# Seven of eight experts taken by rank of their token counts, each place with its own number of rows

## The chip, the cores and the metric

One core of a Trainium2 chip runs the whole program. The time is the device time of one execution in microseconds (us). The engines are PE (matrix products), ACT, DVE and POOL (element-wise work and index work) and SP, which issues most of the DMAs; the profile counts loads of PE's weights apart, as PEld. The median of three runs before the change is 919.82 us (919.14 to 919.92).

## The reference

Three layers follow each other on 3072 tokens (4 sequences of 768) of 384 values: a linear attention with a decaying state per head, a maximum of three products with an output product, and a mixture of eight experts in which every token goes to two. Cut to the last layer, on which the change works:

```python
noisy = x @ w_gate + log1p(exp(x @ w_noise)) * noise      # 3072 x 8
top2 = the two largest of each row; top2_w = softmax of the two
for e in range(8):
    rows = tokens that have e among their two
    h = maximum(x[rows] @ w1[e], 0)                        # 384 -> 1024
    out[rows] += weight of e * (h @ w2[e])                 # 1024 -> 384
```

With the inputs that setup_inputs() draws, this arithmetic gives the experts 799, 828, 716, 763, 766, 766, 772 and 734 tokens (expert 0 to 7), 6144 in all.

## The kernel before, in words

**The first half.** Attention and the three-product layer run over eight blocks of 384 tokens. After each block a short routing program on DVE finds each token's two experts and its place among their tokens, and six indirect DMAs of POOL (L632) write the token's 393 words (384 values, eight gate weights, its number) to a table in HBM, `XS`. Expert e owns rows 896 e to 896 e + 895 there (`CAP` is 896), and rows that no token takes hold zeros and a number past the end.

**The expert stage.** An expert's rows are done in two groups: g = 0 has its first 512 rows, g = 1 the next 320 (`GR` is 832, so a group of 832 - 512 columns). The list `groups` has the order (0,0), (0,1), (1,0), ... (7,1). The second group's columns are the same for all experts. If an expert has more than 832 rows, a flag is set, and `more_rows` does the rest after the stage.

A group goes through these steps:

- `g_load` (L694, L697): SP loads the rows into `raw`. The second group's load comes as two parts, 128 partitions with two rows each and 64 partitions with one.
- `g_tr` (L709 to L713): PE turns a tile of rows (three 128 x 128 transposes into a `b_sc` bank, of which there are two), ACT copies it rounded as `gxH`, DVE makes the rest `gxL`. Each product is done in three terms (high x high, low x high, high x low), which keeps full precision.
- `g_gate` (L722, L724): DVE copies the row numbers into `gix`, of which there are two buffers, one for each of the last two groups. The weight of the token is read where it lies, in `raw`.
- `mm1` (L734 to L736): for each of eight slices f of the hidden layer nine matmuls fill a `b_u` bank, with the group's columns moving; ACT makes `ghH` (L745), DVE `ghL` (L746). There are two `b_u` banks.
- `mm2` for g = 0 (L762 to L764): per f twelve matmuls, the tokens as weights, 384 columns moving. `mm2T` for g = 1 (L777 to L779): per f nine matmuls with `w2` as weights and the group's columns moving; the result lies turned, and `g_cols` (L788, L790) and `g_rows` (L802) turn it back, the latter inside the next expert's first step. The very last group does its eight `mm1` first and then `mm2_tile` (L815 to L817), 24 matmuls of 384 columns for each of three tiles.
- `g_out` (L827 to L833): ACT and DVE scale by the weight into `ys`, and POOL adds the rows to `out` with an indirect DMA, which reads `gix`.

**The order** is written out by hand in a loop over the groups and f = 0 to 8: `mm1(f)`, then `mm2(f - 1)`, then, from f = 3 on, the turning of one tile of the next group (`g_tr` with j = f - 3), then the conversion `e_conv` (L667 on ACT, L668 on DVE) of a piece of the next expert's weights and the load `e_load` (L654, L657) of the piece three further on; `est` has three buffers. Only the very first group differs: there the next group's rows are loaded at f = 6, its first tile is turned at f = 7 and tiles 1 and 2 at f = 8, behind `mm2(7)`. Every engine takes its instructions in the order of the program, and SP's DMAs too wait in that order. `flags` (L1011 to L1031) is a chain of small DVE operations in the first group of expert 1.

## Time and profile before

| | |
|---|---|
| median of the runs | 919.82 us |
| profiled execution, whole | 925.38 us |
| profiled execution, span of the trace | 923.6 us |
| first half and routing, up to the first expert matmul | 445.3 us |
| expert stage, first to last matmul | 445.35 to 913.50 us |
| one first group in the middle (expert 1) | 35.77 us |
| one second group in the middle (expert 1) | 22.42 us |
| after the last matmul | 10.10 us |
| PE busy over the span | 899.3 us, 97% |
| granted clock of PE, mean | 0.995 |

The profile gives each instruction its start and its duration. For PE the duration of a matmul overlaps that of the next one, so that what a matmul costs is read as the distance from one start to the next, not as its duration. A bracket at the end of a row tells how long the engine had been idle before and what released it.

### The profile page before, as it was taken

Reading aid. Unit: us, or ns where it says so; the run is one execution under the profiler, and the core shown is the slowest. Engines: PE = TensorE matmul, PEld = TensorE weight load, DVE = VectorE, ACT = ScalarE, POOL = GpSimd, SP = SyncE. Lnnn points to the kernel's source line nnn. Section 1 sums busy time; section 2 is a strip of 40 time slices with the busy share of each in tenths; the row PEclk is TensorE's granted clock in tenths of the full one; section 3 lists DMA queues with packets and bytes.
Section 4 is the critical chain, followed back from the end, with each engine's and each line's share of the span. In section 5 each row is a group of like instructions: output and inputs, shape, how many; then the busy total and the mean of one; then the engine's idle time right before and its main releaser. Section 6 shows DMA issues by size and latency. Waiting matters only on the chain.

```text
span 923.6 us, 15940 instructions
## 1 busy us (share of the span) xinstructions
PE 899.3 (97%) x6450; PEld 830.3 (90%) x6451; DVE 500.8 (54%) x1281; ACT 271.7 (29%) x555; POOL 136.5 (15%) x116
## 2 busy tenths in 40 slices
PE   7999999999999999999999999999999999999995
PEld 6767999989999999999989899998999999989895
DVE  8896876758585776747425443343433433434230
ACT  3124422212121222224124333343333433334220
POOL 1000020100202020200131121021210212102121
PEclk9999999999999999999999999999999999999998
DMA  9880332525314141123145453234531435324121
GB/s 296 265 235 2 92 109 79 192 74 170 128 51 145 48 135 40 53 72 101 53 142 139 127 122 95 68 88 109 133 89 57 101 108 138 81 62 104 41 35 18
DMA packets 46211, 96.94 MB, mean 105 GB/s; under 512 B 5937, under 2 KB 26930, under 8 KB 46130
## 3 DMA queue, kind: packets, MB, share of 16 engines
q1 hardware_dynamic: 34962, 75.89, 26.3%
q0 software_dynamic: 10624, 19.11, 9.8%
q8 instruction: 52, 0.85, 0.4%
q10 hardware_dynamic: 544, 0.85, 0.3%
q14 instruction: 29, 0.24, 0.1%
HBM read 68.79 MB, written 27.82 MB: 105 GB/s over the span
## 4 chain that ended last, share of the span: by engine, by line
PE 91%; DVE 5%; issue 2%; ACT 1%; DMA 0%; POOL 0%; POOLq 0%; ACTq 0%; DVEq 0%
PE b_u L549 8%; PE b_u L734 8%; PE b_u L735 8%; PE b_u L736 8%; PE b_u L550 7%; PE b_u L551 7%; PE b_sc L375 2%; PE b_y L399 2%; PE b_sc L709 2%; PE b_y L394 2%; PE b_u L547 2%; PE b_y L762 1%; PE b_tx L764 1%; PE b_st L762 1%; PE b_x L764 1%
## 5 line engine op out<-in xcount | busy, mean ns | idle before, releaser
L746 DVE SCALAR_TENSOR_TENSOR ghL<-b_u,ghH 128x512 fp32r<-128x512 f32 (+1 forms) x120 | 71.6, 597 | 174.7 <-ACT ghH L745 166.3
L734 PE MATMUL b_u<-gxH,e1H 128*128 128x512 f32 (+1 forms) x384 | 140.2, 365 | 0.5 <-ACT gxH L712 0.5
L833 POOL DMA_INDIRECT out_dram<-ys,gix x56 | 86.1, 1538 | 360.6 <-ACT ys L830 334.0
L549 PE MATMUL b_u<-xHt,wH 128*128 128x384 f32 x378 | 133.9, 354 | 3.3 <-issue 3.3
L735 PE MATMUL b_u<-gxL,e1H 128*128 128x512 f32 (+1 forms) x384 | 134.9, 351 | 0.2 <-DVE gxL L713 0.2
L736 PE MATMUL b_u<-gxH,e1L 128*128 128x512 f32 (+1 forms) x384 | 135.1, 352 | 0.0
L551 PE MATMUL b_u<-xHt,wl 128*128 128x384 f32 x378 | 127.5, 337 | 0.0
L550 PE MATMUL b_u<-xLt,wH 128*128 128x384 f32 x378 | 127.4, 337 | 0.0
L745 ACT ACTIVATE ghH<-b_u 128x512 fp32r<-128x512 f32 (+1 forms) x120 | 62.8, 523 | 189.1 <-PE b_u L736 180.0
L632 POOL DMA_INDIRECT XS<-rows,ii x48 | 48.0, 1000 | 418.3 <-ACT xHt L442 299.2
L736 PEld LDWEIGHTS b_u<-gxH,e1L 128*128 128x128 f32 x384 | 72.1, 188 | 8.6
L558 DVE TENSOR_TENSOR uw<-b_u,uw 128x384 f32<-128x384 f32 x96 | 53.4, 556 | 48.7 <-PE b_u L551 37.0
L549 PEld LDWEIGHTS b_u<-xHt,wH 128*128 128x128 f32 x378 | 71.0, 188 | 8.1 <-issue 4.9
L734 PEld LDWEIGHTS b_u<-gxH,e1H 128*128 128x128 f32 x384 | 72.2, 188 | 6.7 <-ACT gxH L712 0.6
L735 PEld LDWEIGHTS b_u<-gxL,e1H 128*128 128x128 f32 x384 | 72.4, 188 | 6.2 <-DVE gxL L713 0.4
L560 ACT ACTIVATE hHt<-uw 128x384 fp32r<-128x384 f32 x48 | 25.2, 525 | 157.5 <-DVE uw L558 127.1
L550 PEld LDWEIGHTS b_u<-xLt,wH 128*128 128x128 f32 x378 | 71.4, 189 | 0.0
L551 PEld LDWEIGHTS b_u<-xHt,wl 128*128 128x128 f32 x378 | 70.9, 187 | 0.0
L713 DVE TENSOR_TENSOR gxL<-b_sc,gxH 128x384 fp32r<-128x384 f32 (+1 forms) x56 | 29.4, 527 | 55.0 <-ACT gxH L712 54.9
L712 ACT ACTIVATE gxH<-b_sc 128x384 fp32r<-128x384 f32 (+1 forms) x56 | 26.1, 468 | 81.3 <-PE b_sc L709 81.3
L554 ACT ACTIVATE uw<-b_u 128x384 f32<-128x384 f32 x48 | 23.5, 489 | 53.1 <-PE b_u L551 46.5
L668 DVE TENSOR_TENSOR e1L<-est,e1H 128x768 fp32r<-128x768 f32 x32 | 30.7, 960 | 9.2 <-ACT e1H L667 8.7
(297 smaller groups left out, 1822.3 us busy)
## 6 DMA issues: line engine op xcount, KB each, us to landing
est<-in_ew_dram SPq DMA_DIRECT2D x64, 384.0 KB
ldt<-in_tm_dram SPq DMA_DIRECT2D x18, 608.0 KB
raw<-XS SPq DMA_DIRECT2D x8, 786.0 KB
wS<-in_w_dram SPq DMA_DIRECT2D x15, 384.0 KB
ldr<-in_rT_dram SPq DMA_DIRECT2D x24, 224.0 KB
ldk<-in_kT_dram SPq DMA_DIRECT2D x22, 224.0 KB
out_dram<-zrow SPq DMA_DIRECT2D x8, 576.0 KB
XS<-zrow SPq DMA_DIRECT2D x8, 393.0 KB
```

Of the source, the lines that this page charges most:

```text
L549: nc.tensor.matmul(o, WH[j][:, f, ks], xH[b][:, k, :], start=(k == 0), stop=False)
L550: nc.tensor.matmul(o, WH[j][:, f, ks], xL[b][:, k, :], start=False, stop=False)
L551: nc.tensor.matmul(o, WL[3 * f + j][:, ks], xH[b][:, k, :], start=False, stop=(k == 2))
L558: v.tensor_tensor(w, o, w, op=OP.max)
L632: st = nc.gpsimd.indirect_dma_start(out=XS, out_offset=bass.IndirectOffsetOnAxis(ap=ii[:, 3 * k + j:3 * k + j + 1], axis=0), in_=rw[:, j, ...
L668: v.tensor_sub(l_, s_, f32(h_))
L734: nc.tensor.matmul(u, a[:, k, fs], o.xH[:, k, :n], start=(k == 0), stop=False)
L735: nc.tensor.matmul(u, a[:, k, fs], o.xL[:, k, :n], start=False, stop=False)
L736: nc.tensor.matmul(u, b[:, k, fs], o.xH[:, k, :n], start=False, stop=(k == 2))
L745: nc.scalar.activation(hH[:, :n], u, AF.Relu)
L746: v.scalar_tensor_tensor(hL[:, :n], u, 0.0, f32(hH[:, :n]), op0=OP.max, op1=OP.subtract)
L833: st = nc.gpsimd.indirect_dma_start(out=out, out_offset=bass.IndirectOffsetOnAxis(ap=o.ix[P, j, :], axis=0), in_=ys[P], in_offset=None, bo ...
```

## The change

`GR` goes. `CAPS` gives each place in the order of work its own number of rows: place 0 is always expert 0 with 816; places 1 to 7 are the other seven experts sorted by falling count, with 848, 816, 800, 784, 784, 768 and 768. The second groups so have 304, 336, 304, 288, 272, 272, 256 and 256 columns in place of 320. Eight small DVE operations (`ranks`) sort the counts at the end of the routing and leave the expert of each place as a number in `nti`; SP loads it into a register, and the DMAs of weights and rows of places 1 to 7 take their address from it. As the program no longer knows which of the eight gate weights is its own, `g_gate` picks it with a product with a one-hot row (`Hot`) and a sum, into a tile `ggt`; `raw` is then not read by `g_out` any more, save for place 0. `gix` has three buffers in place of two. A second group's rows come as two equal parts where there are at most 256, else as 128, 128 and the rest. In the first group tiles 1 and 2 of the next group are turned ahead of `mm2(7)` and not behind it. On SP the load of a place's number, which waits for DVE's `nti`, stands ahead of the place's first three weight loads, and a register instruction ahead of each load. The flag for rows left over compares each place with its own number, with six small operations where one stood.

```diff
@@
 G0 = 512
 LO = 640
-GR = 832
+
+CAPS = (816, 848, 816, 800, 784, 784, 768, 768)
...
+    eidx = consts.tile([128, E], F32, name="eidx")
+    nc.gpsimd.iota(eidx, pattern=[[1, E]], base=0, channel_multiplier=0, allow_small_or_imprecise_dtypes=True)
+    capr = consts.tile([1, E], F32, name="capr")
+    for q, n in enumerate(CAPS):
+        nc.gpsimd.memset(capr[:, q:q + 1], n - (CAP - 1.0))
...
+    def ranks():
...
+        v.tensor_sub(key, Rt[:, 1:], eb[:, 0, 1:])
+        v.scalar_tensor_tensor(key, key, float(E), eidx[:, 1:], op0=OP.mult, op1=OP.subtract)
+        v.tensor_tensor(gt, key[:, None, :].to_broadcast(sh), key[:, :, None].to_broadcast(sh), op=OP.is_gt)
+        v.tensor_reduce(rank, gt, axis=AX.X, op=OP.add)
+        v.tensor_tensor(Hot[:, 1:, 1:], rank[:, None, :].to_broadcast(sh), eidx[:, :M, None].to_broadcast(sh),
+                        op=OP.is_equal)
+        v.tensor_mul(gt, Hot[:, 1:, 1:], eidx[:, None, 1:].to_broadcast(sh))
+        v.tensor_reduce(nth, gt, axis=AX.X, op=OP.add)
+        v.tensor_copy(nti[:, 1:], nth[0:1, :])
...
+            SV[e] = nc.values_load(nti[0:1, e:e + 1], engines=[mybir.EngineType.SP], min_val=1, max_val=E - 1,
...
-            nc.sync.dma_start(t.rearrange("p a c -> p (a c)"), ew1[e, i])
+            nc.sync.dma_start(t.rearrange("p a c -> p (a c)"), of(ew1, e)[i])
...
-        return G0 if g == 0 else GR - G0
...
+        return CAPS[e] - G0 if g else G0
+
+    def gparts(e, g):
+
+        if g == 0:
+            return [128] * 4
+        n = gcols(e, g)
+        return [n // 2] * 2 if n <= 256 else [128, 128, n - 256]
...
-        o.gt = o.raw[:, :, DM + e:DM + e + 1]
-        o.ix = pools[0].tile([128, 4, 1], I32, name="gix", bufs=2)
...
+        o.ix = pools[0].tile([128, 4, 1], I32, name="gix", bufs=3)
...
+            v.tensor_scalar(o.ix[:n, js], o.raw[:n, js, ROW - 1:ROW].bitcast(I32), 0.0, None, op0=OP.max)
+            if e:
+                w = [n, js.stop - js.start, E - 1]
+                v.tensor_mul(gh[:n, js, 1:], o.raw[:n, js, DM + 1:DM + E], Hot[:n, None, e, 1:].to_broadcast(w))
+                v.tensor_reduce(o.gt[:n, js], gh[:n, js, 1:], axis=AX.X, op=OP.add)
...
                 if f == 6:
                     drain(rgen)
+                    ranks()
...
+            if i == 0 and f == 8:
+                for j in range(1, len(gparts(*nxt))):
+                    g_tr(*nxt, j)
             if f > 0 and nxt:
                 (mm2T if g else mm2)(e, g, f - 1)
...
-            if nxt and (f >= 3 if i else f >= 7):
-                js = [f - 3] if i else ([0] if f == 7 else [1, 2])
...
+            j = f - (3 if i else 7)
+            if nxt and 0 <= j < (len(gparts(*nxt)) if i else 1):
+                if j == 0:
+                    g_gate(*nxt)
+                g_tr(*nxt, j)
```

On PE, at the end of the first group, before the change: the transposes of tile 0 of the next group, then `mm2(7)`, then tiles 1 and 2, then the next group's `mm1`.

```order
L709 MATMUL b_sc<-ident,raw 128x128 x2
L762 MATMUL b_y<-e2H,ghH 128x384 [waits Activation_49]
...
L764 MATMUL b_x_5256<-e2H,ghL 128x384
L709 MATMUL b_sc<-ident,raw 128x128 [waits PE_49]
L709 MATMUL b_sc<-ident,raw 128x128 x2
L709 MATMUL b_sc<-ident,raw 128x64 [waits DMAHW7_49,DVE_49]
L709 MATMUL b_sc<-ident,raw 128x64 x2
L734 MATMUL b_u<-gxH,e1H 128x320 [waits Activation_49]
```

And the same place after it (L751 is `g_tr`, L810 to L812 `mm2`, L782 `mm1`).

```order
L751 MATMUL b_sc<-ident,raw 128x128 x2
L751 MATMUL b_sc<-ident,raw 128x128 [waits PE_49]
L751 MATMUL b_sc<-ident,raw 128x128 x2
L751 MATMUL b_sc<-ident,raw 128x48 [waits DMAHW7_49,DVE_49]
L751 MATMUL b_sc<-ident,raw 128x48 x2
L810 MATMUL b_y<-e2H,ghH 128x384 [waits Activation_49]
...
L812 MATMUL b_x_5269<-e2H,ghL 128x384
L782 MATMUL b_u<-gxH,e1H 128x304 [waits Activation_49]
```

The six transposes of tiles 1 and 2, with the wait of tile 2 for DVE, have moved from behind the twelve matmuls of `mm2(7)` to ahead of them.

On DVE, in the second group of expert 0, where the row numbers of the next group are taken, before the change:

```order
L746 SCALAR_TENSOR_TENSOR ghL<-b_u,ghH 128x320 [waits Activation_49]
L722 TENSOR_SCALAR gix<-raw 128x4 [waits DMASW3_49,DMASW2_49,DMAHW3_49,DMASW1_49,DMASW0_49]
L713 TENSOR_TENSOR gxL<-b_sc,gxH 128x3x128 [waits Activation_49]
L668 TENSOR_TENSOR e1L<-est,e1H 128x3x256 [waits DMAHW4_49,Activation_49]
L746 SCALAR_TENSOR_TENSOR ghL<-b_u,ghH 128x320 [waits Activation_49]
```

And after it (DMASW are POOL's DMAs, DMAHW those of SP; L768 to L772 is `g_gate`).

```order
L794 SCALAR_TENSOR_TENSOR ghL<-b_u,ghH 128x304 [waits Activation_49]
L768 TENSOR_SCALAR gix<-raw 128x4 [waits DMAHW3_49]
L771 TENSOR_TENSOR ggh<-raw,Hot 128x4x7
L772 TENSOR_REDUCE ggt<-ggh 128x4 [waits DVE_49]
L755 TENSOR_TENSOR gxL<-b_sc,gxH 128x3x128 [waits Activation_49]
L707 TENSOR_TENSOR e1L<-est,e1H 128x3x256 [waits DMAHW4_49,Activation_49]
L794 SCALAR_TENSOR_TENSOR ghL<-b_u,ghH 128x304 [waits Activation_49]
```

The row numbers no longer wait for four DMAs of POOL, and two small operations stand behind them.

## Rows read from the trace of the kernel before

**Rows 1.** The page: busy time by engine (us, share of the span, instructions), and the chain that ended last by engine.

```profile
PE 899.3 (97%) x6450; PEld 830.3 (90%) x6451; DVE 500.8 (54%) x1281; ACT 271.7 (29%) x555; POOL 136.5 (15%) x116
...
PE 91%; DVE 5%; issue 2%; ACT 1%; DMA 0%; POOL 0%; POOLq 0%; ACTq 0%; DVEq 0%
```

**Rows 2.** Busy time by stretch (us, then busy us and instructions of PE, PEld, DVE, ACT, POOL, granted clock, DMA share, GB/s): the second group of expert 0, both groups of expert 1, and what follows the last matmul.

```profile
480.76:505.46 24.70, 23.28 (x156) 22.58 (x157) 14.99 (x26) 12.66 (x23) 6.73 (x4) 1.00 0.55 145
505.46:541.23 35.77, 35.77 (x190) 32.12 (x188) 14.90 (x38) 11.45 (x20) 5.04 (x4) 1.00 0.35 96
541.23:563.65 22.42, 22.42 (x158) 22.40 (x157) 10.65 (x19) 9.09 (x18) 5.64 (x4) 1.00 0.44 104
...
913.50:923.60 10.10, 0.00 (x1) 0.00 (x0) 0.41 (x1) 0.42 (x1) 1.42 (x1) 0.72 0.07 13
```

**Rows 3.** Timeline of PE: the first matmul of nine with 512 columns, the first of twelve with 384 columns that follow, and (second pair) the first of eighteen with 320 columns and the matmul behind them.

```profile
472.84 0.39 PE L734 MATMUL b_u<-gxH,e1H 128*128 128x512 f32 x1
...
474.94 0.34 PE L762 MATMUL b_y<-e2H,ghH 128*128 128x384 f32 x1
...
541.23 0.31 PE L734 MATMUL b_u<-gxH,e1H 128*128 128x320 f32 x1
...
543.87 0.31 PE L777 MATMUL b_y<-ghH,e2H 128*128 128x320 f32 x1
```

**Rows 4.** Timeline of PE in the first half: twelve matmuls with full weights and 16 moving columns, and the next instruction behind them.

```profile
75.24 1.41 PE L526 MATMUL b_x<-wgs,cols 128*128 128x16 f32 x12
76.50 0.53 PE L515 MATMUL b_st<-ident,wol 128*128 128x128 f32 x3
```

**Rows 5.** Timeline of PE, ACT and DVE at the end of the first group: the turning of tile 0, then `mm2(7)`, then tiles 1 and 2, then the next group.

```profile
477.06 0.49 PE L709 MATMUL b_sc<-ident,raw 128*128 128x128 f32 x3
477.30 0.42 PE L762 MATMUL b_y<-e2H,ghH 128*128 128x384 f32 x1
477.56 0.33 PE L763 MATMUL b_y<-e2L,ghH 128*128 128x384 f32 x1
477.58 0.49 ACT L712 ACTIVATE gxH<-b_sc 128x384 fp32r<-128x384 f32 x1 [1.85 <-PE b_sc L709]
478.11 0.56 DVE L713 TENSOR_TENSOR gxL<-b_sc,gxH 128x384 fp32r<-128x384 f32 x1 [1.52 <-ACT gxH L712]
479.47 0.82 PE L709 MATMUL b_sc<-ident,raw 128*128 128x128 f32 x6
480.76 0.41 PE L734 MATMUL b_u<-gxH,e1H 128*128 128x320 f32 x1 [0.47 <-ACT gxH L712]
481.40 0.42 PE L735 MATMUL b_u<-gxL,e1H 128*128 128x320 f32 x1 [0.22 <-DVE gxL L713]
```

**Rows 6.** Timeline of DVE and PE in the second group of expert 0, and the same wait over the whole stage (total us, times, longest us).

```profile
494.79 0.17 DVE L722 TENSOR_SCALAR gix<-raw 128x4 int32<-128x4 int32 x1 [4.34 <-DMA out_dram<-ys,gix]
495.24 0.31 PE L777 MATMUL b_y<-ghH,e2H 128*128 128x320 f32 x1
496.74 0.41 PE L778 MATMUL b_y<-ghL,e2H 128*128 128x320 f32 x1 [1.20 <-DVE ghL L746]
...
DVE gix L722 <- DMA out_dram<-ys,gix: 16.4, 7, 4.3
```

**Rows 7.** What stands between `mm1` and the matmul that needs its result: groups by shape (count, busy us, mean ns); then, in expert 1's second group, the last `ghL` behind a weight conversion and the matmul that reads it; then, in the last group, an evacuation by ACT and DVE and the next but one `mm1`.

```profile
L746 DVE SCALAR_TENSOR_TENSOR ghL<-b_u,ghH 128x512 fp32r<-128x512 f32 x64 | 44.2, 691 | 132.9 <-ACT ghH L745 129.3 <-issue 3.5
L746 DVE SCALAR_TENSOR_TENSOR ghL<-b_u,ghH 128x320 fp32r<-128x320 f32 x56 | 27.4, 489 | 41.8 <-ACT ghH L745 37.0 <-issue 4.7
...
553.59 0.48 DVE L746 SCALAR_TENSOR_TENSOR ghL<-b_u,ghH 128x320 fp32r<-128x320 f32 x1
555.23 0.31 PE L778 MATMUL b_y<-ghL,e2H 128*128 128x320 f32 x1
...
898.65 0.49 DVE L746 SCALAR_TENSOR_TENSOR e1L<-b_u,e1H 128x320 fp32r<-128x320 f32 x1 [0.83 <-ACT e1H L745]
899.30 0.31 PE L734 MATMUL b_u<-gxH,e1H 128*128 128x320 f32 x1
```

**Rows 8.** The end: POOL's last two indirect DMAs; the POOL-queue line of the closing barrier (count, then ns min/median/max, first and last start); POOL's DMA queue (packets, MB, share) from the last of the two on.

```profile
910.46 1.54 POOL L833 DMA_INDIRECT out_dram<-ys,gix  x1 [2.65 <-DVE ys L828]
914.73 1.42 POOL L833 DMA_INDIRECT out_dram<-ys,gix  x1 [2.73 <-DVE ys L828]
...
L1329 POOLq DRAIN  x3: 50/254/6702, 915.6 to 923.3; - x3
...
q0 software_dynamic: 80, 0.00, 0.4%
```

**Rows 9.** Weight loads: SP's issue of the first three pieces for expert 2, and ACT's first conversion for expert 2.

```profile
510.64 1.55 SPq L654 DMA_DIRECT2D est<-in_ew_dram  x3
516.41 0.85 ACT L667 ACTIVATE e1H<-est 128x768 fp32r<-128x768 f32 x1 [0.72 <-DMA est<-in_ew_dram]
```

**Rows 10.** A small DVE operation of the routing (by shape: count, busy us, mean ns), and DVE's idle time ahead of the first group's last `ghL`.

```profile
L613 DVE TENSOR_TENSOR r_pv<-r_M,r_pf 128x48 f32<-128x48 f32 x8 | 1.7, 207 | 0.0
...
475.77 0.69 DVE L746 SCALAR_TENSOR_TENSOR ghL<-b_u,ghH 128x512 fp32r<-128x512 f32 x1 [3.52 <-ACT ghH L745]
```

**Rows 11.** POOL's DMA queue (packets, MB, share) in the stretches in which the second groups of experts 0 and 1 are added to `out`.

```profile
q0 software_dynamic: 368, 0.44, 16.3%
q0 software_dynamic: 368, 0.49, 19.5%
```

More of the change, by code (lines that the diff above doesn't have):

```diff
@@ L643, in moe_kernel, with number, of @@
     pools = {}
+    Hot = consts.tile([128, E, E], F32, name="Hot")
+    nti = consts.tile([1, E], I32, name="nti")
+    SV = {}
+    def ranks():
+        M = E - 1
+        sh = [128, M, M]
+        p = pools[0]
+        key, gt = p.tile([128, M], F32, name="key"), p.tile(sh, F32, name="gt")
+        rank, nth = p.tile([128, M], F32, name="rank"), p.tile([128, M], F32, name="nth")
+        v.tensor_sub(key, Rt[:, 1:], eb[:, 0, 1:])
[7 more added lines that the diff above has]
+        v.tensor_copy(nti[:, 1:], nth[0:1, :])
+    def number(e):
+        if e not in SV:
+            SV[e] = nc.values_load(nti[0:1, e:e + 1], engines=[mybir.EngineType.SP], min_val=1, max_val=E - 1,
+                                   skip_runtime_bounds_check_because="ranks of seven experts")
+        return SV[e]
+    def of(t, e):
+        return t[e] if e == 0 else t[bass.ds(number(e), 1)].rearrange(" ".join("oabcd"[:len(t.shape)]) + " -> " + "(o a) " + " ".join("bcd"[:len(t.shape) - 2]))
+    XE = XS.rearrange("(e r) c -> e r c", e=E)
     def e_alloc(e):
@@ L795, in g_rows @@
         o.y = []
-        for j in range(gtiles(g)):
-            P, s = gpart(g, j), gslice(g, j)
-            n = P.stop
+        for j, n in enumerate(o.n):
+            s = gslice(e, g, j)
             t = bank("x2") if j == 0 else bank("sc", 2)
@@ L801, in g_rows @@
             for k in range(3):
[L802 removed]
+                nc.tensor.transpose(t[:n, k * 128:k * 128 + 128], o.yT[:, k, s], ident)
     def mm2_tile(e, g, j):
@@ L822, in g_out @@
         o = GP[e, g]
-        for j in range(gtiles(g)) if js is None else js:
+        for j in range(len(o.n)) if js is None else js:
             ys = pools[1].tile([128, DM], F32, name="ys", bufs=4)
-            P = gpart(g, j)
+            P = slice(0, o.n[j])
             if js:
@@ L1009, in flags @@
         cn = consts.tile([1, E], F32, name="cn")
+        sn = pools[0].tile([1, E], F32, name="sn")
+        sm = pools[0].tile([1, E - 1, E - 1], F32, name="sm")
         bad = consts.tile([128, 3 * E], BF, name="bad")
@@ L1080, in moe_kernel @@
             continue
-        for j in range(gtiles(g)):
+        for j in range(len(gparts(e, g))):
             mm2_tile(e, g, j)
@@ L1116, in more_rows @@
+        gt = p.tile([128, 1], F32, name="rgt")
+        if e:
+            gh = p.tile([128, E - 1], F32, name="rgh")
+            nc.vector.tensor_mul(gh[:n], x[:n, DM + 1:DM + E], Hot[:n, e, 1:])
+            nc.vector.tensor_reduce(gt[:n], gh[:n], axis=AX.X, op=OP.add)
+        else:
+            nc.vector.tensor_copy(gt[:n], x[:n, DM:DM + 1])
+        q = ps.tile([128, 3, 128], F32, name="rt")
         for k in range(3):
-            nc.tensor.transpose(q[:, k], x[:, k * 128:k * 128 + 128], ident[:n, :n])
@@ L1124, in more_rows @@
             for k in range(3):
-                nc.tensor.matmul(q, w1[:, a, k, c * 128:c * 128 + 128], xT[:, k], start=(k == 0), stop=(k == 2))
-            nc.scalar.activation(h[:, f], q, AF.Relu)
-        y = ps.tile([n, DM], F32, name="ry")
+                nc.tensor.matmul(q[:, :n], w1[:, a, k, c * 128:c * 128 + 128], xT[:, k, :n], start=(k == 0), stop=(k == 2))
+            nc.scalar.activation(h[:, f, :n], q[:, :n], AF.Relu)
+        y = ps.tile([128, DM], F32, name="ry")
         for f in range(8):
-            nc.tensor.matmul(y, h[:, f], w2[:, f], start=(f == 0), stop=(f == 7))
@@ L1130, in more_rows @@
-        nc.vector.tensor_scalar(ys[:, e], y, x[:, DM + e:DM + e + 1], None, op0=OP.mult)
+            nc.tensor.matmul(y[:n], h[:, f, :n], w2[:, f], start=(f == 0), stop=(f == 7))
+        nc.vector.tensor_scalar(ys[:n, e], y[:n], gt[:n], None, op0=OP.mult)
     with tc.For_i(0, N, 128) as i:
@@ L1133, in more_rows @@
         nc.sync.dma_start(o, out[bass.ds(i, 128), :])
-        oh = p.tile([n, E, 128], F32, name="roh")
+        oh = p.tile([128, E, 128], F32, name="roh")
         y = ps.tile([128, DM], F32, name="ry")
         for e in range(E):
-            nc.vector.tensor_scalar(oh[:, e], iot[:, bass.ds(i, 128)], ix[:, e:e + 1], None, op0=OP.is_equal)
-            nc.tensor.matmul(y, oh[:, e], ys[:, e], start=(e == 0), stop=(e == E - 1))
+            n = CAP - CAPS[e]
+            nc.vector.tensor_scalar(oh[:n, e], iot[:n, bass.ds(i, 128)], ix[:n, e:e + 1], None, op0=OP.is_equal)
+            nc.tensor.matmul(y, oh[:n, e], ys[:n, e], start=(e == 0), stop=(e == E - 1))
         nc.vector.tensor_add(o, o, y)
```

119 lines of the change are left out of this document (59 added, 60 removed).

## The prediction

> **What bounds the kernel now.** I read first the page: PE is busy for 97% of the span and makes 91% of the chain that ended last [rows 1]. The reader is to see there that what shortens the kernel has to shorten PE. The busy share doesn't tell whether PE works at its pace or waits a little everywhere, so the stretches came next. In the expert stage, at a granted clock of 1.00, both groups of expert 1 are busy from end to end, 35.77 and 22.42 us; the second group of expert 0 alone has 24.70 us and 1.4 us of them idle [rows 2]. The stage is eight times the same pair of groups, bound by PE's stream of matmuls, with a disturbance in the first pair. Third came PE's timeline, for the price of a matmul by its columns, and last the waits, for the disturbance.
>
> The price is the distance of starts. Nine matmuls of 512 columns take 474.94 - 472.84 = 2.10 us, 233 ns each [rows 3]; the twelve of 384 columns behind them, up to 477.06, 177 ns each [rows 3, 5]; eighteen of 320 columns 2.64 us, 147 ns each [rows 3]. That is 0.456, 0.460 and 0.458 ns a column: in proportion, with nothing fixed on top. The step from 384 to 320 columns alone gives 30 ns for 64 columns (0.47), that from 512 to 384 56 ns for 128 (0.44). I take 0.457 and keep 0.44 to 0.47.
>
> **The change, part by part** (gains positive).
>
> *Fewer columns in the second groups, places 0 to 6.* Against 320 they lose 16, -16, 16, 32, 48, 48 and 64 columns, 208 together. Each column passes through 72 matmuls of `mm1` and 72 of `mm2T`: 208 x 144 x 0.457 ns = +13.7 us (13.2 to 14.1). The narrowest that the trace shows in this form is 320. For 256 the proportion gives 117 ns, and twelve matmuls with full weights and only 16 columns take 105 ns each (1.26 us) [rows 4]: there the weights are the limit, and it lies below 117. So proportion should hold to 256. The other bound is that the spacing never falls below 147 ns; then the narrower places give nothing, and place 1, wider by 16, costs 1.1.
>
> *The last group.* 64 columns fewer in its 72 matmuls of `mm1`: 64 x 72 x 0.457 = +2.1 us (zero at the other bound). Two tiles in place of three: 24 matmuls of 384 columns, 24 x 177 = +4.2 us, whatever the spacing below 384 does.
>
> *Third parts that vanish.* Places 6 and 7 have two tiles: two turnings in, one turning back, three transposes each. Tile 0's three take 477.06 to 477.30, and the matmul behind them 260 ns for 177 [rows 5]: 0.24 + 0.08, about 0.33 each, +1.0 us. The other third parts keep their instructions, with fewer rows.
>
> *Third buffer for row numbers.* In expert 0's second group DVE stood 4.34 us before `gix`, until the DMAs that add the previous rows had read the buffer, and PE then stood 1.50 us between two matmuls that are 0.15 apart otherwise [rows 6]: +1.35. The other six such waits of DVE (12 us in all) fell into slack; that they go is worth nothing. In the new order `gix` waits only for its own rows. What is late next is the weights' conversion and `gxL` on DVE, one of each per step here; by the row of expert 1 below they are about a microsecond ahead of PE.
>
> *Turning two tiles earlier.* Before, `mm1` of the second group stood behind the turning of tiles 1 and 2: from 479.47 six transposes take about 0.5, the first matmul starts at 480.76 and the second 0.64 later, so 0.8 + 0.5 = 1.3 us are lost [rows 5]. Put ahead of `mm2(7)`, the six follow tile 0 at 477.3. But there are two `b_sc` banks, and tile 2 needs the one of tile 0, which DVE reads until 478.67 [rows 5]. PE, which takes its instructions in order, would have tile 1 done at 477.55 and stand until about 478.7, 1.15 us, with `mm2(7)` queued behind. The stall moves rather than goes: +0.1 (-0.3 to 1.3, the latter if PE's wait is met by something earlier).
>
> *Added DVE work.* Eight operations of `ranks` at 0.2 us [rows 10] are 1.6 us; they fall into the 3.52 us in which DVE waits for ACT ahead of its last `ghL` [rows 10]. Five more in `flags` and two to four per group in `g_gate`, 0.4 to 0.8 us, lie in steps of 2.3 to 4.2 us. DVE is busy 10.65 us of 22.42 [rows 2], so no rate is at stake, only how early `ghL` comes. Its tightest steady place is 554.07 to 555.23, 1.16 us [rows 7], and that with `gix` late. At 256 columns the 18 matmuls between take 0.53 us less and `ghL` itself 0.07 less (1.05 ns a column by its two widths): 0.7 in hand, and 0.35 after the gate's two operations. Where nothing lies between, at the last step of a second group and in the last group's `mm1`, the margin is 0.16 us (899.14 to 899.30) [rows 7] and sinks below zero at 256: I count -0.5 for small waits (0 to -2).
>
> *SP and POOL.* SP's load of a number, `nti`, stands ahead of the next place's weights, and they wait for `ranks`; the first such loads come some 2 to 3 us later than before, and are needed only in the second group, from 480.8 on [rows 5]. A place's own row load no longer waits for the scaling of the group before, so later ones come earlier. POOL's nine operations at the start lie long before its first indirect DMA. Nothing counted.
>
> *The end.* The last tile had no live row: after its issue POOL's queue moved 80 packets of next to no bytes [rows 8]. Now the last tile holds about 102 of the 716 - 512 = 204 rows of place 7. If the closing barrier, in which POOL's drain takes 6.7 us [rows 8], waits for them, that costs up to one more DMA's length, 1.5 to 1.9 us; if the drain is fixed, 0.1. I take -0.8.
>
> The sum: 13.7 + 2.1 + 4.2 + 1.0 + 1.35 + 0.1 - 0.5 - 0.8 = 21.15 us. The profiled execution's 925.4 would become 904.2; it stands 5.6 above the median of the runs, which I take as the profiler's own share, so 919.8 becomes 898.7.
>
> A sentence on a rule that speaks against the largest term: the Trainium skill, TensorE: Matmul & The Clock Gate, section "Back-to-back issue gap", gives for a stream of weight loads and matmuls about 81 ns at 128 columns and 131 ns at 512, a slope of 0.13 ns a column; by it the two column terms would be an estimated 4.5 us in place of 15.8, and the time some 910. The trace disagrees at 512 columns, with 233 ns [rows 3], so I go by the trace.
>
> **Rivals.**
>
> *The spacing stops falling* somewhere below 320 columns. For it: no row here has such a matmul between 16 and 320 columns. Against it: proportion to within 1% over three widths, and the 105 ns. At its full price the column terms are -1.1 + 0 and the gain 21.15 - 15.8 - 1.1 = 4.3: 915.5. Chance 0.05. The slope of the Trainium skill, above, would be a milder form of it.
>
> *ACT and DVE become the bound in the narrow groups.* For it: both run in order, and the conversion of weights stays as it was while PE's step shrinks from 2.8 to 2.3 us. Against it: DVE is half busy [rows 2]. If the five groups of 288 and fewer columns lose 0.25 us in each of eight steps, that is 10 us more: about 908. Chance 0.08.
>
> *Slower: loads addressed by a register are slow.* The place is ACT, which in order waits for a weight piece ahead of the next `ghH`; then PE stands. For it: the trace has no such load, and ACT did wait for pieces, though briefly. Against it: three pieces issued at 510.64 behind two row loads were there at 516.41, 5.8 us [rows 9]. With three buffers a piece has three conversions' time from issue to use, six steps of a narrow group, 13.6 us. So it decides from a landing of about 14 us on: eight pieces in threes cost 2.7 x the excess per expert; seven experts eat up the 21 us at about 14.7 us of landing, and at 16 us the time is 919.8 - 21.2 + 2.4 x 2.7 x 7 = 944. Chance 0.03.
>
> *The change doesn't do what it says:* a count exceeds its place, and `more_rows` runs. The counts of the reference, sorted, are 828, 772, 766, 766, 763, 734, 716 for places 1 to 7 and 799 for place 0, all below their numbers; the DMAs of the trace agree, with 0.44 MB and 0.49 MB for the second groups of experts 0 and 1, which are 287 and 316 rows of 1536 bytes [rows 11]. It would load all 64 weight pieces again; at three in 5.8 us [rows 9] that is 120 us: above 1010. Chance 0.01.
>
> **How the numbers follow.** The forecast has 0.83. Its own range: all ends on the good side (14.1 for places 0 to 6, 1.3 for the turning, nothing lost in small waits and 0.1 at the end) give 23.9 and 895.9; all on the bad side (13.2, -0.3, -2, -1.9, 1.2 for the row numbers) 17.5 and 902.3, with the other terms as summed. I give 896 to 904, the upper end a little into the case of the narrow groups. About 0.2%, 1.8 us, is what a measurement of this kernel can tell from no change. Faster by more: the forecast and the first two rivals, 0.96 less a hundredth for their tails, 0.95; slower by more 0.04; within 0.01.
>
> **What would show it.** In the changed profile the second groups should last about 22.4 - 0.066 x (columns lost): 18.2 for 256 columns, with matmuls 117 ns apart. PE should show no wait for `gix` in expert 0's second group, and a new wait of about 1.15 us at the third turning ahead of `mm2(7)`, in place of the two at 480. The last group should have 48 matmuls behind `mm1`, and the stretch behind the last one be 10.1 to 12 us. SP's register loads should land in the 3 to 6 us of before. A spacing above 125 ns at 256 columns, PE waits of over 0.2 us in each narrow step, or ACT waiting for `est` in every group would make the forecast wrong, by the first, second and third rival.

## The result, and the profile after

The changed kernel takes 897.88 us (median of four runs, 897.75 to 899.09), the kernel before, beside it, 919.48: a ratio of 0.9769, 95% interval 0.9752 to 0.9786. Forecast were 898.7 and a range of 896 to 904.

The page of the profile after, first line, busy time and chain, to be held against [rows 1]:

```profile
span 895.8 us, 16084 instructions
...
PE 875.4 (98%) x6417; PEld 808.3 (90%) x6418; DVE 504.6 (56%) x1327; ACT 266.8 (30%) x551; POOL 133.4 (15%) x123
...
PE 91%; DVE 5%; issue 1%; ACT 1%; DMA 0%; POOL 0%; POOLq 0%; ACTq 0%
```

PE has lost 24 us of busy time and still makes 91% of the chain. Nothing new has come into it.

Busy time by stretch (columns as in [rows 2]): the second groups of places 0 (304 columns), 1 (336) and 6 (256), and the first group of place 7:

```profile
474.61:496.25 21.64, 21.58 (x157) 21.34 (x157) 14.25 (x25) 11.92 (x22) 6.24 (x4) 1.00 0.62 166
...
531.91:555.35 23.44, 23.44 (x157) 23.39 (x157) 11.17 (x21) 9.23 (x18) 5.66 (x4) 1.00 0.60 152
...
814.23:832.61 18.38, 18.38 (x157) 18.38 (x157) 10.10 (x20) 8.40 (x18) 5.66 (x4) 1.00 0.61 149
832.61:867.57 34.96, 34.96 (x182) 31.57 (x181) 8.61 (x17) 7.54 (x14) 3.58 (x3) 1.00 0.09 10
```

In each the second column (PE busy) is the stretch itself or 0.06 less: none of these groups waits. That of place 1, wider by 16 columns, is longer than the 22.42 of before, as it must be.

PE's timeline at 256 columns: the first of eighteen matmuls of place 6, and the matmul behind them:

```profile
814.23 0.28 PE L782 MATMUL b_u<-gxH,e1H 128*128 128x256 f32 x1
...
816.34 0.28 PE L825 MATMUL b_y<-ghH,e2H 128*128 128x256 f32 x1
```

2.11 us for eighteen are 117 ns each, the forecast's number.

The turning at the end of the first group, PE and then ACT and DVE, against [rows 5]:

```profile
470.44 0.82 PE L751 MATMUL b_sc<-ident,raw 128*128 128x128 f32 x6
472.11 0.38 PE L751 MATMUL b_sc<-ident,raw 48*128 48x48 f32 x3 [0.85 <-DVE gxL L755]
472.42 0.45 PE L810 MATMUL b_y<-e2H,ghH 128*128 128x384 f32 x1
...
474.61 0.31 PE L782 MATMUL b_u<-gxH,e1H 128*128 128x304 f32 x1
...
470.97 0.87 ACT L754 ACTIVATE gxH<-b_sc 128x384 fp32r<-128x384 f32 x2 [1.84 <-PE b_sc L751]
...
471.49 1.02 DVE L755 TENSOR_TENSOR gxL<-b_sc,gxH 128x384 fp32r<-128x384 f32 x2 [1.51 <-ACT gxH L754]
```

And the one line that the waits view has of PE in the whole expert stage (total us, times, longest us):

```profile
PE b_sc L751 <- DVE gxL L755: 0.8, 1, 0.8
```

The stall has moved as foreseen: the third turning waits for DVE's first `gxL` (from 471.49, half of 1.02 us), with `mm2(7)` queued behind, and the next group then starts without a wait. From the six transposes (some 0.5 us) to 472.11 PE stands about 1.2 us.

The waits view of the expert stage has no more line for `gix`. It also leaves out waits too small for it. They show as distances of starts in the last group's `mm1`:

```profile
869.45 0.28 PE L783 MATMUL b_u<-gxL,e1H 128*128 128x256 f32 x1
869.57 0.28 PE L784 MATMUL b_u<-gxH,e1L 128*128 128x256 f32 x1
869.73 0.39 PE L782 MATMUL b_u<-gxH,e1H 128*128 128x256 f32 x1
869.95 0.28 PE L783 MATMUL b_u<-gxL,e1H 128*128 128x256 f32 x1
...
869.25 0.42 DVE L794 SCALAR_TENSOR_TENSOR e1L<-b_u,e1H 128x256 fp32r<-128x256 f32 x1 [0.86 <-ACT e1H L793]
```

After 869.57 come 0.16 and 0.22 in place of 0.12 twice: `mm1` needs the bank that DVE frees at 869.67. This happens three times (869.57, 871.84, 874.10), 0.42 us together. It is the margin of 0.16 us in [rows 7], gone below zero.

Where the 21.6 us came from, by the traces, between starts of groups. From the first expert matmul to the last group's start: 444.70 us before, 428.79 after, so 15.91. From there to the last matmul's start: 23.12 and 17.06, so 6.06. From there to the end of the span: 10.43 and 11.17, so -0.74. Together 21.23.

The first halves are left out of this. Before's profile reached its first expert matmul at 445.35 us, after's at 438.78; experiment 8 says why that is hardly the change's.

### The profile page after: what moved, and what is told of

The parts are those of the page before. It is cut to its first block, busy times and chain, and to the rows that moved or that the text cites. A ratio compares the mean times of both kernels' runs of the same rounds, so it can differ in the third digit from the quotient of the medians.

```text
span 895.8 us, 16084 instructions
## 1 busy us (share of the span) xinstructions
PE 875.4 (98%) x6417; PEld 808.3 (90%) x6418; DVE 504.6 (56%) x1327; ACT 266.8 (30%) x551; POOL 133.4 (15%) x123
## 3 DMA queue, kind: packets, MB, share of 16 engines
q0 software_dynamic: 10320, 19.10, 10.8%
## 4 chain that ended last, share of the span: by engine, by line
PE 91%; DVE 5%; issue 1%; ACT 1%; DMA 0%; POOL 0%; POOLq 0%; ACTq 0%
PE b_u L555 8%; PE b_u L782 8%; PE b_u L784 8%; PE b_u L783 8%; PE b_u L556 7%; PE b_u L557 7%; PE b_sc L381 2%; PE b_y L405 2%; PE b_sc L751 2%; PE b_y L400 2%; PE b_u L553 2%; PE b_st L810 1%; PE b_st L812 1%; PE b_y L810 1%; PE b_st L811 1%; PE b_y L812 1%
## 5 line engine op out<-in xcount | busy, mean ns | idle before, releaser
L794 DVE SCALAR_TENSOR_TENSOR ghL<-b_u,ghH 128x512 fp32r<-128x512 f32 (+5 forms) x120 | 69.9, 583 | 175.0 <-ACT ghH L793 175.0
L782 PE MATMUL b_u<-gxH,e1H 128*128 128x512 f32 (+5 forms) x384 | 137.2, 357 | 0.0
L880 POOL DMA_INDIRECT out_dram<-ys,gix x54 | 82.2, 1522 | 342.7 <-ACT ys L877 320.9
L784 PE MATMUL b_u<-gxH,e1L 128*128 128x512 f32 (+5 forms) x384 | 132.6, 345 | 0.0
L783 PE MATMUL b_u<-gxL,e1H 128*128 128x512 f32 (+5 forms) x384 | 132.3, 345 | 0.0
L793 ACT ACTIVATE ghH<-b_u 128x512 fp32r<-128x512 f32 (+5 forms) x120 | 61.4, 512 | 191.7 <-PE b_u L784 187.9
L782 PEld LDWEIGHTS b_u<-gxH,e1H 128*128 128x128 f32 x384 | 72.2, 188 | 6.3
L755 DVE TENSOR_TENSOR gxL<-b_sc,gxH 128x384 fp32r<-128x384 f32 (+4 forms) x54 | 28.4, 527 | 53.1 <-ACT gxH L754 53.1
L754 ACT ACTIVATE gxH<-b_sc 128x384 fp32r<-128x384 f32 (+4 forms) x54 | 25.1, 468 | 71.9 <-PE b_sc L751 71.9
L707 DVE TENSOR_TENSOR e2L<-est,e2H 128x768 fp32r<-128x768 f32 x32 | 30.7, 958 | 7.6 <-ACT e2H L706 7.6
```

The lines of the kernel that those rows point to most:

```text
L707: v.tensor_sub(l_, s_, f32(h_))
L782: nc.tensor.matmul(u, a[:, k, fs], o.xH[:, k, :n], start=(k == 0), stop=False)
L783: nc.tensor.matmul(u, a[:, k, fs], o.xL[:, k, :n], start=False, stop=False)
L784: nc.tensor.matmul(u, b[:, k, fs], o.xH[:, k, :n], start=False, stop=(k == 2))
L793: nc.scalar.activation(hH[:, :n], u, AF.Relu)
L794: v.scalar_tensor_tensor(hL[:, :n], u, 0.0, f32(hH[:, :n]), op0=OP.max, op1=OP.subtract)
```

## The experiments

Kernels that were timed together ran on one chip, and the chips differ: before took 921.7 on the first (experiments 1 to 4), 919.4 on the second (5 to 7) and 922.4 on the third (8, 9 and the repetition in 4). The lengths of the groups in the expert stage, however, repeat from profile to profile of the same kernel within 0.05 us. So tenths are read from the groups, and the times are given beside. Between kernels a tenth can also come from something else than the edit, as experiments 2, 7 and 9 show.

**1. All places at 832 rows.**

```diff
-CAPS = (816, 848, 816, 800, 784, 784, 768, 768)
+CAPS = (832,) * 8
...
-        y = o.y[j][:, :DM]
+        y = o.y[j][:o.n[j], :DM]
```

(The second pair lets the last group's third tile, of 64 rows, be written by `mm2_tile`.)

> The changed kernel with every place at 832 rows, so that all second groups have 320 columns and three tiles again, while the ranks, the loads by a register, the third gix buffer and the new place of the turning stay. Theory (the columns, the third tile of the last group and the vanished third parts carry all but about a microsecond of the 21.6 us gained): only gix +1.35 and about +0.3 for the moved stall stay, less up to 0.5 for the added DVE work, so 1 us less than before, 918.0 to 919.0. Rival (the register loads, ranks and gates cost PE something that the narrower groups hide): slower than before, 920 or more. Rival (gix and the turning are worth more than I counted, the columns less): 916 or less.

Measured: 921.53 us, ratio to before 1.0005 (0.9996 to 1.0014). Its stretches, second groups of places 0, 1 and 6 and the first groups of 6 and 7:

```profile
476.75:499.34 22.59, 22.59 (x157) 22.38 (x157) 14.45 (x25) 12.04 (x22) 6.26 (x4) 1.00 0.62 159
...
535.27:557.66 22.39, 22.39 (x157) 22.36 (x157) 11.01 (x21) 9.09 (x18) 5.64 (x4) 1.00 0.64 161
...
790.46:826.26 35.80, 35.80 (x188) 32.09 (x187) 12.83 (x24) 11.33 (x20) 5.00 (x4) 1.00 0.26 58
826.26:848.68 22.42, 22.42 (x158) 22.39 (x157) 11.02 (x21) 9.11 (x18) 5.71 (x4) 1.00 0.52 127
848.68:884.47 35.79, 35.79 (x189) 32.12 (x187) 8.99 (x20) 8.41 (x16) 5.05 (x4) 1.00 0.08 10
```

The time shows nothing left without the columns. In the trace 1.1 us are: the stage from the first expert matmul to the last group takes 443.56 us, 1.14 less than before, but the end of the span is 11.70 us behind the last matmul, 1.27 more. Set against after, group by group, the second groups of places 0 to 6 give 0.95, -1.05, 1.09, 2.04, 3.04, 3.03 and 4.04 us (place 6: 22.42 to 18.38), 13.1 in all, or 0.44 ns a column and matmul. The first groups of places 6 and 7, with one and two third parts less, give 0.50 and 0.83 us. So the columns carry the change. The ranks, register loads and gates cost nothing that PE shows: the stage with them is no longer than with the third buffer alone (443.86 us, experiment 2).

**2. The third buffer alone**, in the kernel before.

```diff
-        o.ix = pools[0].tile([128, 4, 1], I32, name="gix", bufs=2)
+        o.ix = pools[0].tile([128, 4, 1], I32, name="gix", bufs=3)
```

> The kernel before with a third gix buffer alone. Theory: PE's pause of 1.50 us in the second group of expert 0 goes and the other six waits of DVE were slack, so 1.35 us less than before: 918.1, ratio 0.9985. Rival (the pause only moves to the next wait, on ghL or on a weight's conversion): no difference, 919.5.

Measured: 920.49 us, ratio 0.9995 (0.998 to 1.001), which by itself tells neither from the other. The two groups of expert 0 and the first of expert 1:

```profile
442.75:478.12 35.37, 34.90 (x180) 31.05 (x179) 13.30 (x62) 7.23 (x15) 5.82 (x6) 1.00 0.25 86
478.12:501.36 23.24, 23.01 (x157) 22.57 (x158) 15.20 (x26) 12.68 (x23) 7.53 (x4) 1.00 0.59 154
501.36:537.27 35.91, 35.91 (x189) 32.07 (x188) 14.92 (x38) 11.46 (x20) 5.05 (x4) 1.00 0.36 95
```

The pause is worth 1.46 us (24.70 to 23.24). But each later first group takes about 0.1 us more than before (35.91 for 35.77, then 35.78 to 35.84 for 35.66 to 35.73), with PE busy throughout. The stage as a whole takes 443.86 us against 444.70, a gain of 0.84 us. Neither theory had that. The buffer takes away DVE's waits, and it may also move the tiles allocated around it. Which of the two costs the tenth was not tried, but waits are not needed for such a difference: in before itself the first groups of experts 2, 4 and 6 take 35.73 us and those of experts 3, 5 and 7 35.67, with the same instructions and their weights in another pool.

**3. The turning put back.**

```diff
-            if i == 0 and f == 8:
-                for j in range(1, len(gparts(*nxt))):
-                    g_tr(*nxt, j)
             if f > 0 and nxt:
                 (mm2T if g else mm2)(e, g, f - 1)
+            if i == 0 and f == 8:
+                for j in range(1, len(gparts(*nxt))):
+                    g_tr(*nxt, j)
```

> The changed kernel with the turning of tiles 1 and 2 behind mm2(7) again. Theory (the stall only moved: about 1.2 us of PE standing at the third turning now, 1.3 us of two waits at the next group's start before): within 0.4 us of the changed kernel, 897.5 to 898.3, the wait at the third turning gone and waits for gxH and gxL of some 1 us together back. Rival (the move itself is worth its 1.3 us, and the wait seen at the third turning costs nothing): 899.2.

Measured: 900.94 us, ratio 0.9776 (0.9763 to 0.9788). The changed kernel wasn't timed beside it, so the groups of expert 0 decide:

```profile
442.05:477.39 35.34, 34.90 (x181) 31.07 (x180) 14.72 (x70) 7.16 (x15) 5.83 (x6) 1.00 0.25 86
477.39:499.61 22.22, 21.95 (x157) 21.48 (x157) 15.24 (x28) 12.55 (x23) 7.25 (x4) 1.00 0.60 161
```

PE's waits in them:

```profile
PE b_u L782 <- ACT gxH L754: 0.4, 1, 0.4
PE b_u L783 <- DVE gxL L755: 0.2, 1, 0.2
```

Both groups of expert 0 take 57.56 us, after 35.83 + 21.64 = 57.47. The waits of before are back, the one at the third turning is gone, and the move is worth 0.09 us.

**4. `mm2(7)` cut around the third turning.**

```diff
...
             if i == 0 and f == 8:
-                for j in range(1, len(gparts(*nxt))):
-                    g_tr(*nxt, j)
+                g_tr(*nxt, 1)
+                mm2(e, g, 7, (0, 1))
+                if len(gparts(*nxt)) == 3:
+                    g_tr(*nxt, 2)
+                mm2(e, g, 7, (2, 3))
-            if f > 0 and nxt:
+            elif f > 0 and nxt:
                 (mm2T if g else mm2)(e, g, f - 1)
```

(`mm2` takes the tiles that it multiplies as a last argument.)

> The changed kernel with mm2(7) cut in two: tile 1 is turned ahead of it, then come its tiles 0 and 1 (six matmuls, 1.06 us), then tile 2 is turned, then its tiles 2 and 3. Theory (the third turning waits for DVE to free the bank of tile 0, which takes about 1.2 us from the second turning on): the six matmuls cover the wait but for 0.1 us, and the six behind them cover the copies of tile 2, so 1.1 us less than the changed kernel: 896.8. Rival (DVE and ACT, not the bank, are what is late: the wait turns up at the next group's first matmuls): no difference, 897.9.

Measured: 899.46 us, ratio 0.977 (0.9756 to 0.9784). PE's timeline at the third turning:

```profile
472.79 0.82 PE L751 MATMUL b_sc<-ident,raw 128*128 128x128 f32 x6
473.36 0.42 PE L810 MATMUL b_y<-e2H,ghH 128*128 128x384 f32 x1
...
474.60 0.39 PE L751 MATMUL b_sc<-ident,raw 48*128 48x48 f32 x3
474.92 0.44 PE L810 MATMUL b_tx<-e2H,ghH 128*128 128x384 f32 x1
...
476.07 0.31 PE L782 MATMUL b_u<-gxH,e1H 128*128 128x304 f32 x1
```

And the stretch of expert 0's first group:

```profile
441.12:476.07 34.95, 34.95 (x181) 31.14 (x180) 15.70 (x72) 7.86 (x16) 5.83 (x6) 1.00 0.26 87
```

The stall is gone: the six matmuls of `mm2(7)` stand where PE stood, and the group takes 34.95 us, busy throughout, for 35.83. Beside the changed kernel, on one chip, it was run again:

> The changed kernel, as the measure for the two below on the same chip: 897.5 to 898.5 if the chip runs the kernel before at 919.5.

> The changed kernel with mm2(7) cut around the turning of tile 2, beside the changed kernel on one chip. Theory (from its first profile: the group shrank from 35.83 to 34.95 and nothing came back): 0.9 us less than the changed kernel, in a stage from the first expert matmul to the last group's start of 427.9 us for 428.8.

Measured: 901.14 us for the changed kernel (ratio 0.9771, 0.9754 to 0.9787) and 899.49 with the cut (0.9754, 0.974 to 0.9768). The intervals overlap, so the times alone don't settle it. The traces do: 428.84 and 427.89 us from the first expert matmul to the last group, 0.95 less, as in the first profile of the cut. The bank was what the third turning waited for.

**5. Narrower still.** Widths apart from the limits that the flags compare with:

```diff
+WID = (816, 848, 736, 720, 704, 672, 640, 768)
...
-        return CAPS[e] - G0 if g else G0
+        return WID[e] - G0 if g else G0
...
```

(The rows beyond these widths are left out, so this kernel does less than the reference.)

> The changed kernel with second groups of 304, 336, 224, 208, 192, 160 and 128 columns in places 0 to 6 (two tiles of 64 to 112 rows from 224 on); the rows of places 2 to 6 beyond these are left out. It asks where the proportion ends, 256 columns being the narrowest that the change uses. Theory (proportion down to the floor of 105 ns that full weights with 16 columns showed, so to about 230 columns): all five groups at 144 x 105 ns plus the 1.4 us that the groups of 256 columns have beside their 144 matmuls, 16.5 us each, with spacings of 105 ns. Rival (the proportion goes on, the weights load beside it): 102, 95, 88, 73 and 58 ns, groups of 16.1, 15.1, 14.0, 11.9 and 9.8 us. Rival (ACT and DVE become the bound below 256): groups longer than 144 times the spacing by over 3 us, with waits for ghL in each step. Rival (narrow matmuls cost more): spacings above 118 ns.

Measured: one run of 882.6 us, with the second groups of 224, 208, 192, 160 and 128 columns at 17.40, 17.34, 17.29, 17.26 and 17.23 us. The two ends of that:

```profile
590.97:608.37 17.40, 17.40 (x157) 17.40 (x157) 9.72 (x20) 8.17 (x18) 5.66 (x4) 1.00 0.77 198
...
800.29:817.52 17.23, 17.23 (x157) 17.23 (x157) 9.03 (x20) 7.44 (x18) 5.70 (x4) 1.00 0.65 160
```

PE's timeline, the first two of eighteen matmuls of 128 columns and the one behind them; then, in the kernel before, the last three of the twelve of [rows 4], and 32 matmuls with 64 columns of weights and 48 moving:

```profile
800.29 0.22 PE L783 MATMUL b_u<-gxH,e1H 128*128 128x128 f32 x1
800.35 0.28 PE L784 MATMUL b_u<-gxL,e1H 128*128 128x128 f32 x1
...
802.25 0.27 PE L826 MATMUL b_y<-ghH,e2H 128*128 128x128 f32 x1
...
76.16 0.49 PE L526 MATMUL b_x<-wgs,cols 128*128 128x16 f32 x3
76.50 0.31 PE L515 MATMUL b_st<-ident,wol 128*128 128x128 f32 x1
...
11.12 1.14 PE L399 MATMUL b_y<-cols,A 128*64 128x48 f32 x32
12.09 0.57 PE L407 MATMUL b_st<-cols,K 128*64 128x48 f32 x15
```

There is a floor, and it lies at 112 ns. All eighteen take 1.96 us, which is 109 each, but the first step is only 60 ns long; the other seventeen take 1.90 us (802.25 - 800.35), 112 each, and so do those of 224 columns. The 105 that I read from sixteen columns holds a first step of 28 ns too; its last three take 0.34 us, 112 or 113 each. So a group can give 1.0 to 1.15 us below its 18.38 at 256 columns and no more, and the proportion ends at 240 to 245 columns (from 18.38 by 0.063 us a column down to 17.40, or 112 / 0.457). The narrowest place of the change stands just above. ACT and DVE bound none of these groups, even at 128 columns: PE is busy throughout.

That the floor is the weights' is argued and not tried by itself. PEld's busy time doesn't show it, since PEld is busy for 22.40 of 22.42 us at 320 columns as well [rows 2]. What speaks for it: with 128 columns of weights the spacing is the same for 16, 128 and 224 moving columns, and a fixed price of a matmul it is not, since with 64 columns of weights 32 matmuls take 0.97 us (12.09 - 11.12), 30 ns each. The Trainium skill, TensorE: Matmul & The Clock Gate, section "LDWEIGHTS (loading the stationary operand)", gives columns / 1.2 ns, an estimated 107 for 128; the trace, with 112, is 5% above it. The section "Back-to-back issue gap" of that page of the Trainium skill gives about 81 ns for 128 moving columns, which doesn't hold for this stream (112).

**6. Loads from fixed addresses.**

```diff
-        return t[e] if e == 0 else t[bass.ds(number(e), 1)].rearrange(...)
+        return t[(0, 1, 6, 4, 5, 3, 7, 2)[e]]
```

> The changed kernel with the order of the experts written in (0, 1, 6, 4, 5, 3, 7, 2, which is the order of the reference's counts), so that rows and weights are loaded from fixed addresses; the ranks are still computed for the gates. Theory (loads by a register land as early as fixed ones, and those that come later fall into slack): within 0.3 us of the changed kernel run beside it. Rival (the registers' reads on SP, 0.3 to 0.6 us each, and the later first loads of expert 2's place cost PE time): 0.5 to 2 us less than the changed kernel.

> The changed kernel itself once more, beside the others on one chip, with a profile of its own. Theory (the 6.6 us by which the first half of the profile of before is longer belong to that one execution): its first half ends within 3 us of the other profiles, 438 to 443 us, and its groups take what they took in the first profile, within 0.05 us each. Rival (the change made something in the first half faster): 438.8 again and again, against 441 to 445 for kernels without it.

Measured, on one chip: 898.10 us with fixed addresses (ratio 0.9772, 0.9758 to 0.9785), 897.79 for the changed kernel (0.9763, 0.975 to 0.9776). That is 0.3 us more without the registers, inside the spread of either; all groups of the two agree within 0.02 us. The registers cost nothing here: SP waits 1.8 us once, for `nti`, and ACT waits for a weight piece 0.2 us in the whole stage, where it waited six times and 4.9 us before. The page of the profile after has the weight pieces at 3.2 us from issue to landing, in the median (8.3 at most):

```profile
est<-in_ew_dram SPq DMA_DIRECT2D x64, 384.0 KB, 3.2
```

**7. A last tile that writes nothing.**

```diff
+    dead = consts.tile([128, 1], I32, name="dead")
+    nc.gpsimd.iota(dead, pattern=[[0, 1]], base=N, channel_multiplier=1)
...
-... bass.IndirectOffsetOnAxis(ap=o.ix[P, j, :], axis=0),
+... bass.IndirectOffsetOnAxis(ap=dead if js == [1] else o.ix[P, j, :], axis=0),
```

(The rows of the last tile are left out of the result.)

> The changed kernel with dead row numbers for the last tile, so that POOL's last indirect DMA writes nothing; the rows of that tile are left out. Theory (the closing barrier waits for the rows that the last DMA adds): from the last matmul's end to the end of the span 10.1 us in place of 10.8, the length before. Rival (the barrier's drain is fixed): 10.8 again.

Measured: one run of 897.81 us. From the last matmul's start to the end of the span 10.86 us pass, against 11.17 to 11.46 in the nine other profiles with rows of the reference in that tile. Before has 10.43, 10.27 a second time, and 10.62 with three buffers; the kernel of experiment 1, whose last tile is dead as well, has 11.70. By these lengths neither expectation holds. But a length holds more than the drain. POOL's last DMA after and here, then the drain of the barrier after, here and in experiment 1, against [rows 8]:

```profile
886.16 1.54 POOL L880 DMA_INDIRECT out_dram<-ys,gix  x1 [2.58 <-DVE ys L875]
...
887.05 1.54 POOL L882 DMA_INDIRECT out_dram<-ys,dead  x1 [3.14 <-DVE ys L877]
```

```profile
L1393 POOLq DRAIN  x3: 50/255/7431, 887.1 to 895.5; - x3
...
L1395 POOLq DRAIN  x3: 50/174/6712, 888.0 to 895.6; - x3
...
L1393 POOLq DRAIN  x3: 50/107/5377, 913.0 to 918.9; - x3
```

Here the last DMA starts 2.01 us behind the last matmul's start (885.04), after 1.52 (884.63), and that hides half a microsecond. The drain itself settles it: it starts 0.9 us behind the start of the DMA in both, and takes 6.71 us without the rows against 7.43 to 7.73 in the nine profiles with them. Before, whose last tile is dead too, has 6.70 [rows 8], 6.51 a second time and 6.84 with three buffers. So the rows lengthen the drain by 0.6 to 1.2 us. The 11.70 of experiment 1 is no witness against it: there the drain takes 5.38 us and starts 5.5 us behind the last matmul's start (907.50) in place of 2.4 to 2.9. Why it starts late there, no view shows.

The groups ahead of that tile are a finding by themselves. Their instructions are those of after, and their lengths repeat from one profile of after to the next within 0.02 us; here, with a constant tile of 4 bytes a partition more, they are from 0.16 us shorter (first group of place 3: 35.66 for 35.82) to 0.13 longer. The second group of place 6, 18.38 after:

```profile
814.48:832.95 18.47, 18.47 (x157) 18.47 (x157) 10.08 (x20) 8.40 (x18) 5.66 (x4) 1.00 0.61 149
```

**8. Before once more.**

> The kernel before once more, for a second profile of it. Theory (the 5.6 us by which its first profile stood above the median were a disturbance in the first half of that one execution): its first expert matmul starts at 438 to 441 us in place of 445.35, the span is 917 to 919, and the groups repeat to 0.05 us, the first groups of experts 1 to 7 at 35.7, where every kernel with a third gix buffer showed 35.8. Rival (what a profile adds is added each time): a span of 923 again. Of the first groups: if they show 35.8 here, the 0.1 us per expert by which the other kernels are longer belong to the execution and not to the kernel.

Measured: one run of 922.07 us, on a chip whose median for it is 922.4. The first two groups:

```profile
442.21:477.62 35.41, 34.94 (x180) 31.12 (x179) 13.31 (x62) 7.22 (x15) 5.84 (x6) 1.00 0.26 86
477.62:502.28 24.66, 23.27 (x157) 22.58 (x157) 14.93 (x26) 12.68 (x23) 7.51 (x4) 1.00 0.56 145
```

The first expert matmul starts at 442.21 us, later than the 438 to 441 expected; the changed kernel on the same chip has 442.22, with the cut 441.19, and the kernel of experiment 9 441.65. On the second chip four kernels have 438.86 to 439.16, on the first chip four have 440.91 to 442.75. So the first half differs from chip to chip and by up to 1.9 us on one chip, and the 445.35 of the first profile was that one execution's. A few tenths of the change's own in the first half are not excluded: the medians of before and after differ by 21.6, 21.6 and 21.3 us on three occasions, where the traces have 21.2 behind the first expert matmul. The profiled runs stand near their medians (897.75 to 897.88, 922.07 to 922.4; 922.05 to 920.49 with three buffers is the farthest of the rest): a profile as such doesn't add 5.6 us. The later first groups are 35.66 to 35.81 again, for 35.78 to 35.91 with three buffers; the tenth belongs to the kernel, and its cause stays open.

**9. Places just above the counts**, with the cut of experiment 4. A draw of tokens with a count above its place would pay `more_rows`.

```diff
-CAPS = (816, 848, 816, 800, 784, 784, 768, 768)
+CAPS = (800, 832, 784, 768, 768, 768, 768, 768)
```

> The kernel with the cut mm2(7) and places of 800, 832, 784, 768, 768, 768, 768 and 768 rows, each just above its count here. That takes 128 columns more out of the second groups and three third parts more. Theory (the columns at the 0.439 ns that the runs so far gave, 128 x 144 x 0.439 = 8.1 us, the third parts at the 0.44 us that they measured, 6 x 0.44 = 2.7): 10.7 us less than with the cut alone, 886.3 where the changed kernel has 897.9. Rival (some small waits on ghL come up as more groups have 256 columns): 888 or more.

Measured: 890.32 us (888.98 to 890.62), ratio to before 0.9649 (0.9635 to 0.9664), where the changed kernel had 901.14: 10.8 us less than that, 9.2 less than with the cut alone. The second groups of places 2 and 3:

```profile
591.49:610.92 19.43, 19.43 (x158) 19.43 (x157) 10.32 (x21) 8.56 (x18) 5.70 (x4) 1.00 0.72 181
...
646.18:664.69 18.51, 18.51 (x158) 18.51 (x158) 10.10 (x20) 8.38 (x18) 5.66 (x4) 1.00 0.73 190
```

PE's only wait in the expert stage:

```profile
PE b_y L826 <- DVE ghL L794: 0.2, 1, 0.2
```

The stage shrinks from 427.89 to 418.31 us, 9.6 for an expected 10.7. It is not the rival's waits (0.2 us) that make the difference: the second groups give 7.2 us for 8.1 and the first groups 2.4 for 2.7, and a group of 256 columns takes 18.47 to 18.51 here, 0.1 more than in after. Why, no view shows. The width alone it is not, since in experiment 7 the same group with the same width takes 18.47.

## Why the prediction was right

- *Columns, places 0 to 6*: 13.7 predicted, 13.1 measured (experiment 1). Proportion held down to 256 columns: 117 ns over the first eighteen, 118 to 119 in the median of the whole group. The first rival, a spacing that stops falling below 320, is out, though a floor does lie at 112 ns. The 105 that I used [rows 4] was misread by a first step of 28 ns; the argument had 12 ns of room and in truth 5.
- *The last group*: `mm1` 2.1 less my 0.5 for small waits, together 1.6; measured 10.58 to 8.91, 1.67, with three waits of 0.14 on the bank. That is where I had put them, by the margin of [rows 7]. The third tile was 4.2, measured 4.4 (12.54 to 8.15 from the first such matmul to the last). In the narrow second groups the small waits didn't come, even at 128 columns; so the second rival is out too.
- *Third parts that vanish*: 1.0, measured 1.33 in three, 0.44 each.
- *Third buffer*: 1.35, measured 1.46 for the pause and 0.84 for the stage. The step that failed is "they fell into slack; that they go is worth nothing": with the buffer the first groups of experts 1 to 7 grew by a tenth each. It is a loss of 0.6 that I hadn't counted. Its mechanism is not shown; that the waits are gone needn't be it, as experiment 7 has differences of the same size with no wait of PE changed.
- *Turning two tiles earlier*: +0.1, measured +0.09, by the very stall named: 1.15 us at the third turning forecast, about 1.2 seen.
- *Ranks, gates, registers*: nothing, and nothing seen (experiments 1 and 6). The rival of the slow loads is out: a weight piece lands 3.2 us after its issue in the median and 8.3 at most, where 14 would have been needed. And no count exceeded its place, which would have shown as over 1010 us.
- *The end*: -0.8, measured -0.74 between the two profiles. The step held: the closing barrier waits for the rows, by a drain of 7.43 us for 6.70, and without the rows it is 6.71 (experiment 7).

These measured terms add up to 13.1 + 1.67 + 4.4 + 1.33 + 0.84 + 0.09 - 0.74 = 20.7, for 21.23 in the traces and 21.15 predicted; the other half microsecond is not assigned. 0.27 of it is the first group of place 1, 35.66 us after and 35.93 in experiment 1. That the total came within half a microsecond is in part luck: the columns and the third buffer were put 0.6 and 0.5 too high, and the third parts, the third tile and what is not assigned make up for it.

One step was wrong without harm: "which I take as the profiler's own share", of the 5.6 us by which the profiled run stood above the median. They were one execution's first half (experiment 8). Taking them off was right all the same, since the change doesn't touch that half; had I scaled by them or looked for the change in them, it would have gone wrong.

## What to carry to other kernels

Where PE is busy from end to end, the price of a matmul read as the distance of starts, at two or three widths, forecasts a change of widths to a few per cent; look for the floor (here 112 ns, at 240 to 245 columns) before cutting further, and leave the first step of a run out of its average. A stall at a bank can be covered with matmuls that don't need the bank: cut the step behind it and put half of it in between. Before comparing two profiles, compare the stretch that the change doesn't touch, and set apart what differs there.

## What the runs showed of the hardware that was not expected

With 128 columns of weights the spacing has one floor, 112 ns, for 16, 128 and 224 moving columns alike (experiment 5). And streams of the same matmuls, with PE busy throughout, differ by tenths from kernel to kernel: 0.1 us more in some 36 with a third buffer of 16 bytes a partition, in both kernels that have it and still 320 columns (experiments 1 and 2), and from 0.16 less to 0.13 more with a constant tile of 4 bytes a partition (experiment 7). Within one kernel they repeat to 0.05. That it depends on where the tiles lie is a guess that fits all of these; no run tested it.
